# Moving the squares of four pairs of heads to other slots of ScalarE's order, in hash attention followed by a channel mix

## The chip, the core and the metric

The kernel runs on one core of one Trainium2 chip. The metric is the device time of one execution in microseconds. In this document PE is TensorE (matmuls), ACT is ScalarE, DVE is VectorE, POOL is GpSimd, and SP is SyncE, which only issues transfers. A name with q behind it (SPq, ACTq) is an engine's sequencer.

## The reference

Two layers follow one another. The first is attention over 4 batches of 8 heads, 768 positions and 64 features, in which a query sees only those keys that fall in the same hash bucket (6 sign bits of a projection):

```python
q_bits = (np.einsum('bhsd,dk->bhsk', q, proj) > 0).astype(np.int64)
k_bits = (np.einsum('bhsd,dk->bhsk', k, proj) > 0).astype(np.int64)
...
mask = q_bucket[:, :, :, None] == k_bucket[:, :, None, :]
scores = scale * np.matmul(q, k.transpose(0, 1, 3, 2))
scores = np.where(mask, scores, -1000000000.0)
...
return np.matmul(attn, v).astype(np.float32)
```

Between them stands a softmax over the keys. The second layer is a channel mix (here "the feed-forward") on the attention output, with 512 model features and 1024 hidden ones:

```python
xk = mu_k * x + (1.0 - mu_k) * x_prev
xr = mu_r * x + (1.0 - mu_r) * x_prev
k = np.maximum(xk @ w_k, 0.0)
v = k * k @ w_v
r = 1.0 / (1.0 + np.exp(-(xr @ w_r)))
return (r * v).astype(np.float32)
```

x_prev is x shifted by one position.

## The kernel before

The 32 heads are worked on as 16 pairs, four pairs to a batch. A pair has 12 *slots*: two heads times six chunks of 128 keys. The loop over G walks through all 192 slots; pair n and slot s are `divmod(G, 12)`. The order of the instructions on every engine is the order in which this loop emits them, so each engine's queue is fixed by hand.

In each slot the loop emits, in this order:

- `score`: two matmuls (line 487) of 128 keys against all 768 queries into one of two score buffers in PSUM, and one exp on ACT (line 494) that reads it and gives the chunk P. The sign bits of the hash are extra rows of the same matmul, and the exp's bias lets only chunks of equal buckets survive.
- `pv`: six matmuls (line 515) of the chunk P of two slots before with V, into an accumulator that one head holds in PSUM; ahead of a head's first ones stands one more matmul (line 506). After a head's last chunk DVE divides (lines 526 and 527). Where that chunk is a head's first, `pv` comes at the end of the slot.
- one half of the slot's share of the feed-forward (`ffn(rate / 2)`).
- `outputs` (transposes of the finished pair in slot 3, the mixing of x and x_prev on DVE from slot 4), `prepare` (transposes and casts of a later pair in slots 8 and 9, its sign bits in slot 11) and then `squares`.
- the second half of the feed-forward's share.

The feed-forward of a batch is a queue of matmuls, cut so that it lasts for the 48 slots of the next batch's pairs. It is filled at the end of slot 6 of each batch's first pair (pairs 4, 8 and 12; the last batch's runs behind the loop). First come the k groups of four matmuls (line 584, tile kp), each closed by a relu, which in slots 2, 5 and 6 runs on DVE and in all others on ACT (line 615), and a product on DVE (line 621). After some 19 slots come the groups rp of four matmuls, each closed by a tanh on ACT (line 632), and vp of eight, closed by a product on DVE with that tanh (line 642) and a store. A batch's last pair, n = 7, 11 or 15, therefore has tanhs and no relus on ACT.

Score buffers are two. All other accumulators share four PSUM banks, which `take` hands out in the order in which `give` returned them.

`squares` is a check beside the main path. For every pair from 4 on, ACT squares the raw block of q (index 0) and of k (index 1) with a sum for each partition, by `norm` (line 310), each as one activation over 128x768 elements and one read of the accumulator. The sums go to `nrm`, and at the very end `check_bound` tests their maximum against a bound; only if that fails is the slow general path run. The raw blocks lie in three buffers, so the load of pair n + 3 (`load_blocks`, line 277), which SP issues in slot 10 of pair n, waits for both squares of pair n. The squares of pairs 0 to 3 are made behind the loop.

Of the kernel before, what the change touches and what calls it, by code (L numbers as in the profile page):

```python
# [36 lines left out]
def kernel(  # L37
# [13 lines left out]
    nc = tc.nc  # L51
# [8 lines left out]
    NPB = H // 2  # L60
    NPAIRS = B * NPB
    NTE = 4
# [105 lines left out]
    def fast():  # L168
        with ExitStack() as fx:
# [129 lines left out]
            def norm(n, i, eng):  # L299

                if n < NTE:
                    src = nats[n][:, i].rearrange("p j f -> p (j f)")
                    shape = [P, S]
                else:
                    src = blks[n][:, i].rearrange("p f (c x) -> p (f c) x", x=D)[:, :, 0 : D // 2]
                    shape = [P, 4 * NC_, D // 2]
                junk = junkp.tile(shape, BF16, name=f"sq{n}_{i}", tag="sq")
                acc = nrm[:, 2 * n + i : 2 * n + i + 1]
                if eng is nc.scalar:
                    nc.scalar.activation(junk, src, AF.Square, accum_out=acc)  # L310
                else:
                    eng.scalar_tensor_tensor(
                        out=junk, in0=src, scalar=1.0, in1=src, op0=ALU.mult, op1=ALU.mult,
                        accum_out=acc,
                    )
# [582 lines left out]
                    pieces.pop(0)()  # L898

            def squares(n, s):  # L900
                if n >= NTE and s in (5, 9):
                    norm(n, s // 9, nc.scalar)

# [49 lines left out]
            for G in range(nslots + LAG):  # L955
                clock[0] = G
                n, s = divmod(G, 12)
# [16 lines left out]
                if live:  # L974
                    outputs(n, s)
                    prepare(n, s)
                    squares(n, s)
                    if n and s in (1, 2) and n + 1 < NPAIRS:
                        values(n + 1, s - 1)
# [252 lines left out]
```

## Time and profile before

| | |
|---|---|
| median of three runs | 252.36 us (251.42 to 252.36) |
| profiled execution | 252.61 us, of which the span of the trace is 250.8 us |
| PE, ACT, DVE, POOL busy | 96%, 83%, 67%, 45% of the span |
| mean granted TensorE clock | 0.996 |
| exp on ACT (line 494) | 192, mean 813 ns |
| squares of blocks on ACT (line 310) | 24, 841 ns with little spread, and 24 reads of the accumulator of about 0.19 us |
| relu on ACT (line 615) | 50, mean 498 ns |
| tanh on ACT (line 632) | 24, mean 593 ns |
| pairs 5 to 14, from the first scores of one to those of the next | 13.3 to 14.6 us |

The table gives durations of single instructions. On ACT one instruction begins before the one ahead of it has written everything, so the time from start to start is shorter than the duration. Matmul ends are modelled, their starts are recorded; PE's waits are therefore read from starts. A group of consecutive instructions is merged into one line of a timeline, with its count.

Pair 4 begins at 48 us, pair 7 at 89 us, pair 11 at 146 us and pair 15 at 202 us; the loop ends at 217 us, and the last batch's feed-forward runs on to the end.

### The profile page before, as it was taken

To read this page: it belongs to the slowest core of one execution; us is meant where nothing else is said; L and a number is where in the kernel's file an instruction comes from. 1 tells how busy PE (TensorE), PEld (TensorE's weight loads), DVE (VectorE), ACT (ScalarE), POOL (GpSimd) and SP (SyncE) were. 2 spreads that over 40 slices of the span, in tenths; PEclk is the share of its full clock that TensorE was granted. 3 is DMA by queue.
4 is the path that set the end of the run, shared out by engine and by line. 5 is a ranking of instruction groups with operands and counts; after the bars stand their busy time and mean duration, and the time that the engine had idled before them with its cause. 6 is when DMAs were issued, how large, how long until landed. Compare 5 with 4: busy or idle time off the path is not lost.

```text
span 250.8 us, 6650 instructions
## 1 busy us (share of the span) xinstructions
PE 241.8 (96%) x2422; PEld 146.6 (58%) x2444; DVE 166.8 (67%) x389; ACT 208.6 (83%) x344; POOL 113.6 (45%) x214
## 2 busy tenths in 40 slices
PE   8999999999999999999999999999999999999993
PEld 5566666566656555565656555565666565555442
DVE  2787887876787738575787738376687527299421
ACT  4899999999999978889999978889999998639510
POOL 5889776797646371816437270915528000000000
PEclk9999999999999999999999999999999999999998
DMA  6979789496999384847629395757820111120132
GB/s 206 374 171 236 178 188 197 118 187 172 177 224 205 110 211 121 231 103 222 162 86 216 111 203 157 191 116 206 176 66 6 48 42 42 44 84 4 50 121 92
DMA packets 28231, 36.71 MB, mean 146 GB/s; under 512 B 3216, under 2 KB 25376, under 8 KB 28192
## 3 DMA queue, kind: packets, MB, share of 16 engines
q1 hardware_dynamic: 25744, 33.21, 50.0%
q0 software_dynamic: 2160, 2.62, 6.9%
q8 instruction: 21, 0.34, 0.6%
q10 hardware_dynamic: 288, 0.39, 0.5%
q14 instruction: 18, 0.15, 0.2%
HBM read 31.99 MB, written 6.29 MB: 153 GB/s over the span
## 4 chain that ended last, share of the span: by engine, by line
PE 76%; ACT 12%; issue 4%; DMA 3%; SPq 2%; DVE 2%; ACTq 0%
PE sc L487 20%; PE kp L584 16%; PE vp L584 12%; PE oo L515 10%; ACT pt L494 9%; PE rp L584 6%; DMA out_dram<-os 3%; PE bb L446 3%; PE tp L327 2%; SPq L277 2%; PE oo L506 2%; PE idle L925 1%; PE ot L544 1%; ACT sq L310 1%; ACT th L632 1%
## 5 line engine op out<-in xcount | busy, mean ns | idle before, releaser
L494 ACT ACTIVATE pt<-sc 128x768 bf16<-128x768 f32 x192 | 150.8, 813 | 18.4 <-PE sc L487 16.5
L487 PE MATMUL sc<-aq,ak 70*128 70x384 bf16 (+1 forms) x384 | 93.9, 325 | 2.5 <-ACT pt L494 1.7
L515 PEld LDWEIGHTS <-pt 128*128 128x128 bf16 x1152 | 60.5, 97 | 26.8 <-ACT pt L494 0.9
L515 PE MATMUL oo<-va,pt 128*128 128x65 bf16 x1152 | 66.3, 193 | 0.1
L584 PE MATMUL kp<-xk,wk_sb 128*128 128x384 bf16 x256 | 52.6, 326 | 0.0
L584 PE MATMUL vp<-wv_sb,k 128*128 128x512 bf16 (+1 forms) x184 | 50.4, 369 | 0.6
L487 PEld LDWEIGHTS <-ak 70*128 70x128 bf16 (+1 forms) x384 | 34.3, 97 | 28.2 <-issue 6.5
L389 POOL TENSOR_SCALAR aq<-t 64x768 bf16<-64x768 f32 x24 | 19.8, 826 | 62.7 <-DVE t L384 41.9
L621 DVE TENSOR_TENSOR k<-kr 128x384 bf16<-128x384 bf16 x64 | 27.0, 432 | 13.1 <-ACT kr L615 12.7
L642 DVE SCALAR_TENSOR_TENSOR os<-th,vp 128x512 f32<-128x512 bf16 (+1 forms) x25 | 16.6, 665 | 20.2 <-PE vp L584 14.2
L584 PEld LDWEIGHTS <-wk_sb 128*128 128x128 bf16 x256 | 21.6, 97 | 13.6 <-issue 3.8
L615 ACT ACTIVATE kr<-kp 128x384 bf16<-128x384 f32 x50 | 24.9, 498 | 4.4 <-PE kp L584 4.4
L584 PE MATMUL rp<-wr_sb,xr 128*128 128x512 bf16 x90 | 26.8, 379 | 0.3
L584 PEld LDWEIGHTS <-k 128*128 128x128 bf16 x200 | 16.8, 97 | 10.8 <-issue 1.3
L632 ACT ACTIVATE th<-rp 128x512 bf16<-128x512 f32 x24 | 14.2, 593 | 9.7 <-PE rp L584 7.7
L384 DVE STREAM_TRANSPOSE t<-bl 128x768 f32<-128x768 f32 x24 | 22.3, 957 | 0.0
L389 POOL TENSOR_SCALAR ak<-t 64x768 bf16<-64x768 f32 x24 | 20.1, 837 | 4.8 <-DVE t L384 1.9
L545 DVE COPY xt<-ot 128x768 bf16<-128x768 bf16 x16 | 8.9, 558 | 19.3 <-PE ot L544 19.3
L310 ACT ACTIVATE sq<-bl 128x768 bf16<-128x768 f32 x24 | 20.2, 841 | 0.0
L475 POOL TENSOR_TENSOR s<-vf 128x192 f32<-128x192 f32 x32 | 20.0, 625 | 0.0
L527 DVE SCALAR_TENSOR_TENSOR ob<-oo,rc 128x384 bf16<-128x384 f32 x32 | 17.8, 558 | 1.1
L473 POOL CAST va<-vf 128x384 bf16<-128x384 f32 x32 | 17.0, 532 | 2.6 <-DMA vf<-in_v_dram 1.6
(76 smaller groups left out, 221.9 us busy)
## 6 DMA issues: line engine op xcount, KB each, us to landing
bl<-in_q_dram SPq DMA_DIRECT2D x48, 176.0 KB
bl<-in_k_dram SPq DMA_DIRECT2D x48, 176.0 KB
vf<-in_v_dram SPq DMA_DIRECT2D x15, 384.0 KB
out_dram<-os SPq DMA_DIRECT2D x18, 256.0 KB
out_dram<-os SPq DMA_DIRECT2D x12, 128.0 KB
qk<-in_q_dram SPq DMA_DIRECT2D x3, 384.0 KB
qk<-in_k_dram SPq DMA_DIRECT2D x3, 384.0 KB
wk_sb<-in_moe_w_k_dram POOLq DMA_DIRECT2D x2, 512.0 KB, 7.1
```

What stands on the lines that cost most here:

```text
L310: nc.scalar.activation(junk, src, AF.Square, accum_out=acc)
L384: nc.vector.transpose(t32(n)[:, i].rearrange("p h (c f x) -> p (h c) f x", c=3, f=4), src)
L389: eng.tensor_scalar(out=augs[n % NSET]["qk"[i], j][ROWS[j], :], in0=t32(n)[ROWS[j], i].rearrange("p h y -> p (h y)"), scalar1=(1.0, ALPHA)[i],
L473: nc.gpsimd.tensor_copy(to, of)
L475: nc.gpsimd.tensor_add(s3, vf[:, 0 : 3 * D], vf[:, 3 * D : 6 * D])
L487: nc.tensor.matmul(sc[:, sp, 0:HALF], au["k", j][kr, jc * P : (jc + 1) * P], au["q", j][kr, sp * HALF : (sp + 1) * HALF], start=True, stop ...
L494: nc.scalar.activation(pt.rearrange("p (s q) -> p s q", s=2), sc[:, :, 0:HALF], AF.Exp, bias=EXP_BIAS, scale=SCALE / 2.0 if (n, j) == TWIC ...
L515: nc.tensor.matmul(oo[:, ic, :], pts[n, j, jc][:, ic * P : (ic + 1) * P], vas[n % NSET][j][:, jc, :], start=False, stop=(jc == NC_ - 1 and ...
L527: nc.vector.scalar_tensor_tensor(out=obs[n][:, :, j * D : (j + 1) * D], in0=oo[:, :, 0:D], scalar=ROOT_HALF, in1=rc.to_broadcast([P, NC_, D]),
L584: nc.tensor.matmul(box["t"], lhs(), rhs(), start=(i == 0), stop=(i == len(mms) - 1))
L615: nc.scalar.activation(kr, kp, AF.Relu)
L621: 1, lambda: nc.vector.tensor_tensor(out=k2, in0=kr, in1=kr, op=ALU.mult)
```

## The change

The slots in which the two squares of a pair are emitted depend on the pair. In pair 4, the fifth, they go from slots 5 and 9 to slots 8 and 9. In pairs 7, 11 and 15, the last of a batch, they go from 5 and 9 to 3 and 8. All other pairs keep 5 and 9. What is computed, and on which engine, stays the same.

```diff
             def squares(n, s):
-                if n >= NTE and s in (5, 9):
-                    norm(n, s // 9, nc.scalar)
+
+                slots = (8, 9) if n == NTE else (3, 8) if n % NPB == NPB - 1 else (5, 9)
+                if n >= NTE and s in slots:
+                    norm(n, slots.index(s), nc.scalar)
```

NTE and NPB are both 4.

## The prediction

> **What bounds the kernel now.** I read the page's totals first, then the chain that ended last, then PE and ACT in order of time where PE stood still. The page:
>
> ```profile
> PE 241.8 (96%) x2422; PEld 146.6 (58%) x2444; DVE 166.8 (67%) x389; ACT 208.6 (83%) x344; POOL 113.6 (45%) x214
> ...
> PE 76%; ACT 12%; issue 4%; DMA 3%; SPq 2%; DVE 2%; ACTq 0%
> ```
>
> PE is busy for 96% and carries 76% of the chain. So a move on ACT pays only where PE stands still for ACT, and then in full, as long as PE stays the bound behind that place. How long PE stood still I take from the starts of its matmuls in the timeline: one 512-column matmul holds PE 0.215 us (three from 211.66 to 212.30), one 384-column k matmul 0.163 us (four from 58.16 to 58.81). From 53 us to the end four starts that wait for ACT are late by over 0.25 us in places next to squares, and a fifth follows at the end of the last pair. PE in pair 11 (columns: start, length of the merged piece, operation, idle before it with its releaser):
>
> ```profile
> 153.84 0.49 PE L487 MATMUL sc<-aq,ak 128*128 128x384 bf16 x2
> 154.17 0.35 PE L515 MATMUL oo<-va,pt 128*128 128x65 bf16 x6
> 154.35 0.59 PE L584 MATMUL vp<-wv_sb,k 128*128 128x512 bf16 x2
> 155.20 0.48 PE L487 MATMUL sc<-aq,ak 128*128 128x384 bf16 x2 [0.26 <-ACT pt L494]
> ```
>
> Two vp matmuls from 154.35 end their hold at 154.78; the scores of slot 8 start at 155.20, so 0.42 us is lost (the 0.26 shown is less, since PE's ends are modelled). Scores go to two buffers, so those of slot 8 wait for the exp of slot 6. ACT says why that exp is late:
>
> ```profile
> 149.90 0.81 ACT L494 ACTIVATE pt<-sc 128x768 bf16<-128x768 f32 x1 [0.52 <-PE sc L487]
> 151.18 0.81 ACT L494 ACTIVATE pt<-sc 128x768 bf16<-128x768 f32 x1 [0.47 <-PE sc L487]
> 152.33 0.81 ACT L494 ACTIVATE pt<-sc 128x768 bf16<-128x768 f32 x1 [0.35 <-PE sc L487]
> 153.04 0.83 ACT L310 ACTIVATE sq<-bl 128x768 bf16<-128x768 f32 x1
> ...
> 153.86 0.59 ACT L632 ACTIVATE th<-rp 128x512 bf16<-128x512 f32 x1
> 154.34 2.25 ACT L494 ACTIVATE pt<-sc 128x768 bf16<-128x768 f32 x3
> ```
>
> Exps of slots 3, 4, 5; then in slot 5 a square and a tanh one behind the other; then the exp of slot 6, whose scores had been there since about 153.3. Before slots 3, 4 and 5 ACT is idle 0.52, 0.47 and 0.35 us. Pair 7 has the same pattern (square 96.01, tanh 96.84, exp 97.31; scores at 98.17 instead of 97.75), and so has pair 15 (211.33 instead of 210.91).
>
> In pair 4 there is no feed-forward work before slot 7, so a square in slot 5 stands alone in the way, and PE waits behind it:
>
> ```profile
> 54.35 0.81 PE L584 MATMUL kp<-xk,wk_sb 128*128 128x384 bf16 x4
> 55.50 0.48 PE L487 MATMUL sc<-aq,ak 128*128 128x384 bf16 x2 [0.34 <-ACT pt L494]
> ```
>
> Four k matmuls from 54.35 end at 55.00; the scores start at 55.50: 0.50 us.
>
> **The change, part by part.** No instruction is added or removed; seven of the 24 squares change their place in ACT's order. ACT's steps, start to start with work waiting: exp 0.70 (154.34 to 155.03), relu 0.37 (57.95 to 58.32), square with its accumulator read 0.84 (53.82 to 54.66), tanh 0.48 (153.86 to 154.34). An exp starts 0.59 after its scores (155.20 to 155.78) and ends 0.81 after its start; PE starts 0.05 after that.
>
> *Last pairs, first square, slot 5 to 3 (pairs 7, 11, 15).* In pair 11: exp 149.90, square 150.60, next exp 151.44 instead of 151.18, ending 152.25. Its next users on PE are the scores of slot 6 at 152.69, so the delay of 0.26 is hidden; without that cover it would cost 0.26 each. The exp of slot 5 has its scores only for 152.33, as before. Then tanh 153.04, exp of slot 6 at 153.52 instead of 154.34, ending 154.33: the scores of slot 8 need it at 154.78. The 0.42 goes, with 0.40 to spare. Nothing else stands between; DVE's product for the output waits for this tanh, which starts 0.8 earlier. Three pairs: 3 x 0.42 = 1.26 us, price between 0 (all comes back) and 1.26; I take 1.26.
>
> *Last pairs, second square, slot 9 to 8.* In pair 11 the exp of slot 8 then starts at 155.37, the square at 156.07, and the exp of slot 9 at 156.91 rather than about 156.7 when its scores are there. It ends 157.72; the scores of slot 11 start at 158.61 less 0.42 = 158.19. Hidden, by 0.4. At the end of pair 15 it pays, because there exps run late behind this square and a tanh, and the last P times V matmuls wait:
>
> ```profile
> 215.87 0.81 PE L584 MATMUL vp<-wv_sb,k 128*128 128x512 bf16 x3
> 216.81 0.36 PE L515 MATMUL oo<-va,pt 128*128 128x65 bf16 x6
> ```
>
> Three matmuls end at 216.51, so 0.30 is lost. After the change: exp of slot 8 at 211.50, square 212.20, exps 213.04 and 213.76, tanh 214.46, last exp 214.94, ending 215.75; PE asks for it at 216.51 - 0.42 = 216.09. I take 0.30 (0 to 0.30).
>
> *Loads behind the second square.* SP's block loads for pairs 10 and 14 wait for it (SP queue waits for squares 20.6 us in 8 waits), and queued behind them are sign rows and output stores. They may go up to about 1.4 us earlier; their data is needed a pair later, so 0. Pair 15 loads nothing.
>
> *Pair 4, slot 5 to 8.* PE gains 0.50 at 55.50. But the square comes back among relus: from there ACT runs without a gap. Stepping on: exps of slots 6, 7 at 53.73, 54.44; relu 55.27 (0.43 after its last matmul began); exp 55.64, square 56.34, exp 57.18, relu 57.88, square 58.25, exp 59.09, third relu 59.79, ending 60.28 (before: 60.34). PE's scores of slots 8 to 11 would start 0.50 earlier, at 55.00, 56.16, 57.16, 58.31; the exps two slots before end by 57.99 at the latest, so they hold. The fifth k group, first matmul 60.52 before and 60.02 now, takes by the order of `take` and `give` the bank that the third relu empties, at 60.33. So 0.31 of the 0.50 comes back and 0.2 is left. Bounds: 0.50 gained if no bank binds, 0.1 lost if added semaphore instructions (0.04 each) delay that relu; I take 0.2. SP's load behind the second square keeps its time.
>
> The Trainium skill, "ScalarE: Activation LUTs", section "What ACT_TABLE_LOAD costs", gives 186 ns + 0.833 ns an element, less 93 ns of overlap: 0.73 us for such a step. The trace's 0.84 disagrees; by the page pair 4 would be worth 0.4 and the sum 2.0.
>
> Sum: 1.26 + 0.30 + 0.2 = 1.76 us. From 61 us on PE has no other wait near a moved square, and the tail is PE's. The profiled execution took 252.61 (span 250.8 and 1.8 around it) and would take 250.85; the median run is 252.36, 0.25 below it, and gives 250.6.
>
> **Rivals.** *Stalls come back* (0.20): with PE 0.42 earlier, the next late thing is the exp of slot 9 behind its square, or a bank that DVE empties: in pair 11 its block transpose (155.33 to 156.30) holds back its product for the output, which gains 0.17, not 0.42. For: both margins are of the size of the gain. Against: that bank is not asked for before 159.0. The three 0.42 would go, 0.5 stay: 251.9.
>
> *Slower* (0.06): the square stands for a transfer. The chain of waits has, in pair 11:
>
> ```profile
> 147.81 4.63 DMA out_dram<-os
> 152.45 0.10 issue
> ```
>
> and next the square; in pair 7 a store ends at 95.99 just before the square at 96.01. Block loads and stores share eight semaphores. If the square's wait were met only by those stores, ACT would hold it in slot 3, with the exps of slots 4 and 5 behind. Pair 7: square 96.01, exp of slot 4 96.85, ending 97.66, scores of slot 6 at 97.71 instead of 95.88: 1.83 lost, 0.42 saved. Pair 11: exp 153.31, ending 154.12, scores 154.17 instead of 152.69: 1.48 lost, 0.42 saved. With 0.42, 0.30 and 0.2 gained elsewhere: +1.55, so 253.9. It decides from a release 0.6 us after 93.57 (pair 7) or 0.4 after 150.60 (pair 11). Against: pair 7's square ran at ACT's own pace, 0.71 after an exp at 95.30, with a sign transfer on one of its semaphores issued only at 95.47; and its data was issued at 59 to 63. The Trainium skill, "DMA: Bandwidth & Descriptors", section "Why a DMA increments its semaphore by 16 and not by 1", says of two transfers in flight on one semaphore that the later can satisfy the earlier's wait too soon; by that a shared count errs early, not late.
>
> *Nothing moves* (0.04), if timed runs lack these stalls: 252.4.
>
> **How the numbers follow.** Main case 0.70. A measurement tells about 0.5% here, 1.26 us (the three runs span 0.94), so the line is 251.1. The main case lies 0.5 beyond it: 0.64 faster, 0.06 within. The second rival gives 0.02 faster and 0.18 same, the slower one 0.06, the last 0.04 same. Faster 0.66, same 0.28, slower 0.06. Range: 249.6 (the lowest run, 251.42, less 1.76, rounded) to 252.0, which takes in the stalls that come back; out stay the slower case, the last and edges.
>
> **What would show it.** Right: scores of slot 8 in pairs 7, 11, 15 start 0.43 after two vp matmuls, with no idle for ACT; ACT's idle before slots 4 and 5 shrinks; pair 4 keeps a wait of about 0.3 before its fifth k group; no wait before the last P times V. Wrong: a square in slot 3 that starts later than 0.71 after its exp, or new PE idle in slots 6 or 9 to 11 of those pairs.

## The result, and the profile after

The changed kernel takes 250.63 us (median of 10 runs, 249.9 to 251.98) against 252.40 us (10 runs, 251.38 to 253.46): ratio 0.9933, 95% interval 0.9911 to 0.9954. The profiled execution has a span of 248.5 us instead of 250.8. The two lines of its page that answer to those shown before:

```profile
PE 240.3 (97%) x2422; PEld 145.9 (59%) x2444; DVE 167.7 (67%) x389; ACT 208.6 (84%) x344; POOL 113.5 (46%) x214
...
PE 85%; ACT 8%; DMA 4%; issue 1%; SPq 1%; DVE 0%; ACTq 0%
```

Both engines have the same instructions and ACT the same busy time; what fell is ACT's share of the chain, 12% to 8%. In pair 11 ACT now runs like this (start, length, operation, idle before):

```profile
148.94 0.81 ACT L494 ACTIVATE pt<-sc 128x768 bf16<-128x768 f32 x1 [0.52 <-PE sc L487]
149.65 0.84 ACT L310 ACTIVATE sq<-bl 128x768 bf16<-128x768 f32 x1
150.38 0.19 ACT L310 ACTIVATION_READ_ACCUMULATOR sq<-bl 128x1 f32 x1
150.47 1.71 ACT L494 ACTIVATE pt<-sc 128x768 bf16<-128x768 f32 x2
152.08 0.59 ACT L632 ACTIVATE th<-rp 128x512 bf16<-128x512 f32 x1
152.56 2.66 ACT L494 ACTIVATE pt<-sc 128x768 bf16<-128x768 f32 x3
155.12 0.83 ACT L310 ACTIVATE sq<-bl 128x768 bf16<-128x768 f32 x1
```

The square sits in slot 3, for the most part in time in which ACT had been idle: the exp behind it starts 1.53 us after the one ahead of it (148.94 to 150.47), where this took 1.28 before (149.90 to 151.18). In slot 5 the tanh stands alone between exps. PE's scores of slot 8 follow the two vp matmuls after 0.43 us, without a wait:

```profile
153.40 0.59 PE L584 MATMUL vp<-wv_sb,k 128*128 128x512 bf16 x2
153.83 0.49 PE L487 MATMUL sc<-aq,ak 128*128 128x384 bf16 x2
```

At the end of pair 15 the last P times V matmuls follow the three vp matmuls after 0.65 us, as long as those hold PE:

```profile
214.08 0.81 PE L584 MATMUL vp<-wv_sb,k 128*128 128x512 bf16 x3
214.73 0.35 PE L515 MATMUL oo<-va,pt 128*128 128x65 bf16 x6
```

In pair 4 the wait has moved from the scores of slot 8 to a k matmul, and its releaser is now a relu:

```profile
59.22 0.34 PE L584 MATMUL kp<-xk,wk_sb 128*128 128x384 bf16 x1
59.75 0.32 PE L584 MATMUL kp<-xk,wk_sb 128*128 128x384 bf16 x1 [0.19 <-ACT kr L615]
```

To place the gain I cut PE's time at the first scores of pairs, and at the end of the last matmul. All numbers are us from the traces; "around" is what lies before the first scores and behind the last matmul, together.

| kernel | pairs 0-3 | 4 | 5, 6 | 7 | 8-10 | 11 | 12-14 | 15 to the end of PE | around |
|---|---|---|---|---|---|---|---|---|---|
| before | 39.76 | 12.63 | 28.37 | 14.35 | 42.47 | 14.56 | 41.57 | 44.50 | 12.55 |
| changed | 39.36 | 12.53 | 28.36 | 14.14 | 42.47 | 14.14 | 41.58 | 43.77 | 12.17 |

The stretches with moved squares give 0.10 + 0.21 + 0.42 + 0.73 = 1.46 us. Stretches between them agree within 0.01. The other 0.8 of the 2.2 us between the spans lies in the first four pairs and around, where no square was moved.

### The profile page after: what moved, and what is told of

Same layout as the page of the kernel before. It is cut to its first block, busy times and chain, and to the rows that moved or that the text cites. A ratio compares the mean times of both kernels' runs of the same rounds, so it can differ in the third digit from the quotient of the medians.

```text
span 248.5 us, 6652 instructions
## 1 busy us (share of the span) xinstructions
PE 240.3 (97%) x2422; PEld 145.9 (59%) x2444; DVE 167.7 (67%) x389; ACT 208.6 (84%) x344; POOL 113.5 (46%) x214
## 4 chain that ended last, share of the span: by engine, by line
PE 85%; ACT 8%; DMA 4%; issue 1%; SPq 1%; DVE 0%; ACTq 0%
PE sc L487 23%; PE vp L584 16%; PE kp L584 16%; PE oo L515 12%; PE rp L584 8%; ACT pt L494 7%; PE bb L446 3%; DMA qk<-in_q_dram 2%; PE tp L327 2%; PE oo L506 2%; PE ot L544 2%; DMA aq<-sg 2%; PE bb L419 1%; ACT kr L615 0%; ACT sq L310 0%
## 5 line engine op out<-in xcount | busy, mean ns | idle before, releaser
L621 DVE TENSOR_TENSOR k<-kr 128x384 bf16<-128x384 bf16 x64 | 28.5, 455 | 11.7 <-ACT kr L615 11.2
```

The source lines that it names most:

```text
L621: 1, lambda: nc.vector.tensor_tensor(out=k2, in0=kr, in1=kr, op=ALU.mult)
```

## Experiments

Theory of the stalled exp: a square ahead of a tanh delays the exp that PE's next scores need, and moving it into ACT's idle time gives PE that time back. The rival: the stalls come back at the next limit, and the gain has another source, such as the earlier block loads.

**The last pairs alone.**

```diff
-slots = (8, 9) if n == NTE else (3, 8) if n % NPB == NPB - 1 else (5, 9)
+slots = (3, 8) if n % NPB == NPB - 1 else (5, 9)
```

> Only pairs 7, 11 and 15 changed (slots 3 and 8), pair 4 keeps 5 and 9. Measure: from the first scores of a pair to those of the next, on PE (before: pair 4 12.63, pair 7 14.35, pair 11 14.56 us; pair 15 to the end of the last matmul 44.50). Theory of the stalled exp: pair 7 14.14, pair 11 14.14, pair 15 to the end 43.77, pair 4 still 12.63; together 1.36 us less, so a ratio near 0.9946 to the kernel before. Rival (the stalls come back once PE is earlier, and the gain comes from elsewhere): the three stretches keep their length and the ratio is 1.00.

Measured: ratio 0.9937 (0.9907 to 0.9966). Pair 7 14.14, pair 11 14.14, pair 15 to the end 43.78, pair 4 12.62. The last pairs carry 1.35 of the 1.46 us.

**The fifth pair alone.**

```diff
+slots = (8, 9) if n == NTE else (5, 9)
```

> Only pair 4 changed (slots 8 and 9), the last pairs keep 5 and 9. Theory of the stalled exp: pair 4 takes 12.53 instead of 12.63 us, pairs 7, 11 and 15 stay at 14.35, 14.56 and 44.50; 0.1 us, too little for the timed runs, ratio 0.998 to 1.002. Rival: if the pair that opens the feed-forward carried the change, the ratio would be near 0.994.

Measured: ratio 1.0001 (0.9974 to 1.0029). Pair 4 12.53; pairs 7 and 11 14.35 and 14.56, pair 15 to the end 44.51. The two parts add up, stretch by stretch.

**A double dose: both squares in slot 5 of the last pairs.**

```diff
+slots = (5, 5) if n % NPB == NPB - 1 else (5, 9)
```

with a loop over both indices, so that both are emitted.

> Double dose: in pairs 7, 11 and 15 both squares stand in slot 5, pair 4 and all others in 5 and 9. Theory of the stalled exp: the exp of slot 6 comes another 0.84 us later and PE has no slack left there, so pair 7 takes 14.35 + 0.84 = 15.19, pair 11 15.40 us; pair 15 to the end gains 0.84 and loses the wait of 0.30 at its end, 45.04. Together +2.2 us, ratio 1.009. Rival (PE's loss in slot 5 is hidden by other work or is the tanh's, not the square's): no stretch grows by more than 0.2 us.

Measured: ratio 1.0081 (1.0053 to 1.0110). Pair 7 15.32, pair 11 15.53, pair 15 to the end 45.17, together 2.61 us more. ACT in pair 11, and PE's wait behind it:

```profile
153.67 0.84 ACT L310 ACTIVATE sq<-bl 128x768 bf16<-128x768 f32 x1
154.40 0.19 ACT L310 ACTIVATION_READ_ACCUMULATOR sq<-bl 128x1 f32 x1
154.62 0.84 ACT L310 ACTIVATE sq<-bl 128x768 bf16<-128x768 f32 x1
155.38 0.19 ACT L310 ACTIVATION_READ_ACCUMULATOR sq<-bl 128x1 f32 x1
155.47 0.58 ACT L632 ACTIVATE th<-rp 128x512 bf16<-128x512 f32 x1
```

```profile
154.98 0.59 PE L584 MATMUL vp<-wv_sb,k 128*128 128x512 bf16 x2
156.80 0.48 PE L487 MATMUL sc<-aq,ak 128*128 128x384 bf16 x2 [1.22 <-ACT pt L494]
```

The second square lengthens pairs 7 and 11 by 0.97 us each, all of it PE's: there is no slack left in that place. Pair 15 grows by the same 0.97 less the 0.30 that its end no longer loses. The 0.97 is 0.13 more than the 0.84 expected, because the second of two neighbouring squares starts 0.95 after the first (153.67 to 154.62): it follows the read of the accumulator by 0.22, where the tanh follows the second read by 0.09.

**No squares.** The function returns at once, and the sums of pairs 4 to 15 are set to zero ahead of the test of the bound.

```diff
+return
...
+nc.vector.memset(nrm[:, 2 * NTE :], 0.0)
```

> The squares of pairs 4 to 15 are left out (their sums are set to zero, so the bound is tested on pairs 0 to 3 only). It bounds what any placement can give. Theory of the stalled exp: the squares of the last pairs already cost nothing in the changed kernel, so pairs 7 and 11 take 14.14 and pair 15 to the end 43.77 as there; only pair 4 still pays, and falls from 12.53 to about 12.1 us. Ratio to the kernel before near 0.9925. Rival (moved squares still cost PE time in slots 3 and 8, or by the loads that wait for them): pairs 7 and 11 fall below 14.0 us and the ratio is 0.990 or less.

Measured: ratio 0.9916 (0.9883 to 0.9949). Pairs 7 and 11 14.14, pair 15 to the end 43.78, the same as with the moved squares; pair 4 12.12. In the last pairs the six squares now cost nothing that PE shows, and no other placement can give more there. All other pairs keep their lengths too (5 and 6 28.37, 8 to 10 42.47, 12 to 14 41.58), so the squares that were never moved cost PE nothing either. Pair 4 still paid 0.41 us.

**The first square of the last pairs alone.**

```diff
+slots = (3, 9) if n % NPB == NPB - 1 else (5, 9)
```

> Only the first square of pairs 7, 11 and 15 moved (slots 3 and 9), pair 4 keeps 5 and 9. Stretches on PE, from the first scores of a pair to those of the next. Theory of the stalled exp: the waits of slot 8 go, pair 7 14.14 and pair 11 14.14 us; the wait of 0.30 at the end of pair 15 is the second square's and stays, so pair 15 to the end of the last matmul takes 44.50 - 0.42 = 44.08. Together 1.05 us less, ratio 0.996. Rival (both squares have to move, since the second one stands behind the same tanh group): pairs 7 and 11 stay above 14.25.

Measured: pair 7 14.14, pair 11 14.14, pair 15 to the end 44.09, so 1.04 us less in the stretches. The timed ratio is 0.9983 (0.9955 to 1.0010): the expected 0.996 lies at its edge, and by itself it doesn't tell this kernel from the one before. Its profile began late, with the first scores at 9.64 us instead of 8.31, ahead of anything that was changed.

**The second square of the last pairs alone.**

```diff
+slots = (5, 8) if n % NPB == NPB - 1 else (5, 9)
```

> Only the second square of pairs 7, 11 and 15 moved (slots 5 and 8), pair 4 keeps 5 and 9. Theory of the stalled exp: pairs 7 and 11 stay at 14.35 and 14.56 us, pair 15 to the end falls to 44.50 - 0.30 = 44.20, ratio 0.999. Rival (the loads of pairs 10 and 14, which wait for the second square, or its place before slot 9's exp carry part of the gain): pair 7 or 11 falls by 0.1 us or more, or the second square in slot 8, now behind a late exp, adds a wait and they grow.

Measured: pairs 7 and 11 14.35 and 14.56, pair 15 to the end 44.20; ratio 1.0008 (0.9982 to 1.0035). The second square is worth 0.30 at the very end and nothing elsewhere. The block loads of pairs 10 and 14 wait for this square. Counted from the first scores of pairs 7 and 11, they began 0.1 and 1.2 us earlier; no stretch moved by it, so the loads carry none of the gain.

**Where pair 4 loses its 0.41: the relu on DVE.** The changed kernel, with the third k group's relu moved.

```diff
-if (fc % 2 if clock[0] >= 12 * NPAIRS else clock[0] % 12 in (0, 1, 3, 4, 7, 8, 9, 10, 11)):
+if (fc % 2 if clock[0] >= 12 * NPAIRS else clock[0] != 12 * NTE + 10 and clock[0] % 12 in (0, 1, 3, 4, 7, 8, 9, 10, 11)):
```

> The changed kernel with one relu of pair 4, the third k group's in slot 10, on DVE instead of ACT. It tests that the 0.4 us that pair 4 still pays is the fifth k group's wait for the bank that this relu empties behind two squares. Theory: DVE is idle there from about 58 us, the bank is free before PE asks for it, pair 4 falls from 12.53 to about 12.16 us (12.12 without squares) and everything behind it keeps its length; 0.37 us less than the changed kernel, ratio to the kernel before 0.992. Rival (ACT itself is full from the squares on and the next score buffer is late instead): pair 4 stays above 12.4 us.

Measured: pair 4 12.13, all else as in the changed kernel; ratio 0.9923 (0.9894 to 0.9951). On DVE:

```profile
58.62 1.00 DVE L621 TENSOR_TENSOR k<-kr 128x384 bf16<-128x384 bf16 x1 [0.24 <-ACT kr L615]
59.55 0.55 DVE L617 TENSOR_SCALAR kr<-kp 128x384 bf16<-128x384 f32 x1
```

and on PE the two k matmuls behind the sign bits are one piece again:

```profile
60.02 0.50 PE L584 MATMUL kp<-xk,wk_sb 128*128 128x384 bf16 x2
```

The relu ends at 60.10, just ahead of the second of them at 60.20. DVE was done with its transposes at 58.38, but ahead of the relu in its order stands the product of the group before, which waited for ACT's second relu. That product then took 1.00 us, against 0.41 in the kernel before (at 58.59); why is open.

**The same by another way: pair 4's second square on DVE.**

```diff
-norm(n, slots.index(s), nc.scalar)
+norm(n, slots.index(s), nc.vector if (n, s) == (NTE, 9) else nc.scalar)
```

> The changed kernel with the second square of pair 4 (slot 9) on DVE instead of ACT. Theory: ACT reaches the third relu 0.84 us earlier, the bank is free in time, pair 4 falls to about 12.15 us. DVE does the square behind its two block transposes, at an estimated 1.0 us (as long as one transpose of the same block, 0.96), and is idle for 1.4 us there, so nothing behind it waits; ratio to the kernel before 0.992. Rival (the square on DVE holds up the product or the signs behind it, and SP's load waits for it): pair 4 stays at 12.4 us or more, or pair 5 or 6 grows.

Measured: pair 4 12.12, all else as in the changed kernel; ratio 0.9937 (0.9907 to 0.9966). The square took DVE 1.00 us. In both kernels PE has back what pair 4 lost, as with no squares at all. Against the changed kernel that is 0.4 us, or 0.16%, too little for the timed runs, whose intervals overlap that of the changed kernel; the traces show it, the times don't.

## Why the prediction was right, point by point

*PE is the bound from 61 us on, and pays only where it waits for ACT.* Shown: with squares moved, doubled or left out, PE's stretches changed only where a square had delayed an exp or a relu, and the stretches between kept their length within 0.01 us.

*First square, 3 x 0.42 = 1.26.* The mechanism held; one term was mis-sized. Pair 11 gave 0.42; pair 15 gave 0.42 in slot 8 (0.41 in the first-square kernel); pair 7 only 0.21. In pair 7 I counted two vp matmuls ahead of the late scores, as the trace lists them. In the changed kernel it lists two as well (96.57 to 97.22, 0.65 us, the time of three), though the exp two slots before had ended 0.59 us before those scores. So a third matmul's record is missing, and of the 0.42 read before, 0.215 was work. The pages of the kernel before and of the changed kernel say so too: each lists 2422 matmuls (PE) for 2444 weight loads (PEld), while the other eight traces have 2444 of both. In one of those, the kernel with pair 4 alone changed, pair 7 is that of the kernel before. First the kernel before, then that one:

```profile
97.32 0.59 PE L584 MATMUL vp<-wv_sb,k 128*128 128x512 bf16 x2
98.17 0.48 PE L487 MATMUL sc<-aq,ak 128*128 128x384 bf16 x2 [0.26 <-ACT pt L494]
...
97.41 0.81 PE L584 MATMUL vp<-wv_sb,k 128*128 128x512 bf16 x3
98.27 0.49 PE L487 MATMUL sc<-aq,ak 128*128 128x384 bf16 x2
```

Three matmuls of 0.215 from 97.41 end their hold at 98.06, so 0.21 was lost. The whole of the three pairs: 1.05.

*The square is hidden in slot 3.* The exp behind it comes at 150.47, 0.82 after the square, and the scores of slot 6 at 151.74 find its buffer free for 0.46 us. Without squares the pair takes the same 14.14.

*Second square, 0 in the pairs and 0.30 at the end.* Measured 0.30 in the kernel that moves it alone (44.50 to 44.20), and nothing in pairs 7 and 11. Loads: 0, as taken, though in the changed kernel those of pairs 10 and 14 began 0.3 and 1.4 us earlier, counted from the first scores of pairs 7 and 11.

*Pair 4, 0.2 of 0.50.* Measured 0.10. PE's scores of slot 8 did start without waiting, and the rest came back at the fifth k group by the bank that the third relu empties; the two DVE kernels show that this relu is what binds. That it does so by the bank follows from the order of `take` and `give`. The term was mis-sized at two steps. I let the first square follow its exp by 0.70, and it took 0.84, as the trace before had shown for the same square (52.99 to 53.82). In the changed kernel:

```profile
54.94 0.81 ACT L494 ACTIVATE pt<-sc 128x768 bf16<-128x768 f32 x1
55.78 0.84 ACT L310 ACTIVATE sq<-bl 128x768 bf16<-128x768 f32 x1
```

The third relu was to end 0.06 earlier than before, measured from the pair's first scores, and ended at the same 12.27. That is about half of the missing 0.10; a first relu that began 0.07 earlier than in the sum had taken back part of the 0.14. The other half comes behind the third relu: the scores follow that k matmul after 0.21 us (59.75 to 59.96), where it had been 0.16 (60.54 to 60.70).

On the step of a square, the Trainium skill ("ScalarE: Activation LUTs", section "What ACT_TABLE_LOAD costs") would have made pair 4 worth 0.4. Steps of 0.82 to 0.84 measured behind squares, and 0.10 us in that pair, speak against using its figure for an activation that is followed by a read of the accumulator. For the square alone the trace agrees with it: the read starts 0.73 us after the square (149.65 to 150.38), and the exp 0.09 after the read.

*The slower rival* is ruled out: in slot 3 the squares of pairs 7, 11 and 15 start 0.70 to 0.71 after their exps, as those of other pairs do in slot 5. The store that the chain of waits names ahead of pair 11's square was no releaser: in the changed kernel the same store, issued at 146.86, lands at 151.5 to 152.0, and the square starts at 149.65. A link of that chain is inferred, and here the square's own start told better. Of two transfers that share a semaphore the Trainium skill ("DMA: Bandwidth & Descriptors", section "Why a DMA increments its semaphore by 16 and not by 1") says that the wait for the first can pass too soon. No run here shows that; no square here waited too long for such a count either.

*Nothing moves* is ruled out by the interval of the ratio, which ends at 0.9954, and by the stretches.

*Stalls that come back* did so in pair 4 alone, where the prediction had taken it in. In the last pairs the two margins of about 0.4 held: after the change the scores of slots 8 and 11 of pair 11 find their buffers free for 0.45 and 0.50 us.

*The total.* 250.6 forecast, 250.63 measured; the sum was 1.76 and the traces give 1.46 (0.10 less by pair 4, 0.21 by pair 7, both mis-sized upward). The timed difference by the ratio is 1.7 us, 1.2 to 2.2, which holds both. That the median met the forecast so closely is thus partly chance.

## What to carry to other kernels

What side work costs on an engine that is not the bound depends on what stands behind it in that engine's queue. The same square of 0.84 us cost nothing in slot 3, 0.42 or 0.21 in slot 5, and its full length and more (0.97) once the slack there was used up. So look for a slot with idle time ahead of the next result that the bound engine needs, and keep it away from slots that already hold another extra. Cut the bound engine's time at fixed points of the program; such stretches repeat to 0.01 us here and show terms of 0.1 us that timed runs with a spread of some 2 us cannot. Before reading a gap between matmul starts as a wait, check that no record is missing: against the producer's end, and by the counts of matmuls and weight loads on the page.

## What the runs showed of the hardware beyond that

The first square of an execution starts 0.83 to 0.84 us behind its exp in all nine kernels that have it; later ones that follow an exp start after 0.69 to 0.71. In the kernel without squares in the loop, the first one of all follows a relu behind the loop by 0.52, where later ones follow a relu by 0.37 to 0.39. So the first square is about 0.13 late wherever it stands; why is open, and no run tried it. Two squares in a row start 0.95 to 0.96 apart, while an exp follows a square after 0.82 to 0.84. In all ten profiles the time ahead of pair 4 and behind PE's end varies, with no relation to the edit that one profile of each kernel could show: first scores at 8.07 to 9.64 us, pairs 0 to 3 in 39.30 to 40.07, the end behind PE in 3.46 to 4.64. That is of the size of the spread of the timed runs.
